# A gated scan feeding a folded multiplicative FFN: PSUM cut into single banks and pairs, two 256-token chunks in front, squares also on ScalarE, and a new order

## The chip, the cores and the metric

One core of a Trainium2 chip runs the whole kernel in one launch. The metric is the device time of an execution in microseconds (us). TensorE (PE) does the matmuls, VectorE (DVE), ScalarE (ACT) and GpSimd (POOL) the elementwise work, and SyncE (SP) issues nearly all transfers.

## The reference, cut to what matters

Inputs are `x`, `r_gate` and `i_gate` of 4 sequences x 5824 tokens x 256 channels, one parameter per channel, and four weight matrices. All are float32.

```python
a_t     = exp(8 * sigmoid(r_gate) * log(clip(sigmoid(a_param))))
norm    = sqrt(max(1 - a_t * a_t, 1e-6))
x_gated = norm * sigmoid(i_gate) * x
h[t]    = a_t[t] * h[t-1] + x_gated[t]            # along the tokens of a sequence, h = 0 at its start
out     = ((h @ w1) * (h @ w2)) @ w3 @ w_out      # w1, w2: 256x1024, w3: 1024x1024, w_out: 1024x256
```

No nonlinear function stands between `w3` and `w_out`, so the kernel multiplies the two matrices first ("the fold") and uses one 1024x256 matrix afterwards.

## The kernel before, in words

The 23296 tokens go in chunks: one of 256 tokens and then 45 of 512 (`sizes`, L50). For each chunk the following steps are done. The letter is the step's name in the order string, with chunk and half or piece behind it (`a7.2` is step a of chunk 7, piece 2).

- `r`, `i`, `x` (`load`, L118): three transfers of tokens by channels.
- `R`, `I` (L126, L136): tanh on ScalarE, from which the sigmoids are made. `p`, `t` (L142, L146): 1 + tanh, and its product with x, on GpSimd or, in one instruction, on VectorE.
- `V`, `U`: turn both results to channels by tokens, through TensorE (`turn_pe`, L162) for the chunks in `TURN_R` and `TURN_U`, else by a transposing DMA on SP's queue (`turn_dma`, L174).
- `d` (`decay`, L181): Exp on ScalarE, 2 halves of 128 channels. `s` (`square`, L190): a_t squared, on GpSimd, or VectorE for `DV_SQUARE`. `q` (`root`, L197): Sqrt on ScalarE. ScalarE loads another function table when it goes from tanh or Exp to Sqrt and back.
- `g` (`gated`, L202) and `h` (`scan`, L214): on VectorE. `y` (`cast`, L229): h in bf16, on GpSimd, or VectorE for `DV_CAST`.
- `a`, `b` (`up`, L240): the products with w1 and w2 in four pieces of 256 of the 1024 columns. A piece has two output banks of PSUM (`[P, 2, CT]`), four matmuls of 512 tokens.
- `c` (`copy`, L256): brings the first product to SBUF in bf16, a piece of 1024 columns per partition in one instruction, on ScalarE or, for `DV_COPY`, VectorE. `m` (`product`, L262): VectorE multiplies it with the second product, which it reads from PSUM.
- `D` (`down`, L269): 128 tokens, 8 matmuls of 256 columns. `e` (`evac`, L280): output from PSUM, on ScalarE or, for `DV_EVAC`, VectorE. `o` (L294): store.

Beside the chunks stand the weights (`Lw..`, `Cw..`: load and cast), the fold (`Ft`, `Fc`, `Fm`, `Fe`, L328 to L372), warm-up matmuls on the identity (`W`, L235, counts in `WARM`), and the decay parameters (`A0.` to `A2.`, L349 to L366): `la4` is read by one DMA as 128 x 2 single elements, and a dozen instructions of two elements each turn it into the scale of the Exp.

PSUM has eight banks here. Six form three pairs in one pool, which `a` and `b` share; two hold outputs, transposes and the fold:

```python
psum   = ctx.enter_context(tc.tile_pool(name="psum", bufs=3, space=bass.MemoryType.PSUM))
psum_o = ctx.enter_context(tc.tile_pool(name="psum_o", bufs=2, space=bass.MemoryType.PSUM))
```

Nothing is scheduled at run time. `ORDER` (L395) is a string of some 2000 words, and the loop behind it issues the steps in that order. Every engine and SP's queue runs its own instructions in the order of the string, and waits only for the data and buffers that it needs.

Of the kernel before, what the change touches and what calls it, by code (L numbers as in the profile page):

```python
# [22 lines left out]
def kernel(  # L23
# [12 lines left out]
    nc = tc.nc  # L36
# [13 lines left out]
    sizes = [256] + [CT] * 45  # L50
# [10 lines left out]
    psum = ctx.enter_context(tc.tile_pool(name="psum", bufs=3, space=bass.MemoryType.PSUM))  # L61
# [6 lines left out]
    la4 = consts.tile([P, NCB], F32, tag="la4")  # L68
    zz, zd, zt = (consts.tile([P, NCB], F32, name=tag, tag=tag) for tag in ("zz", "zd", "zt"))
# [9 lines left out]
    TURN_R = {0, 1, 2, 3, 4, 5, 7, 8, 13}  # L79
    TURN_U = {0, 1, 2, 3, 5, 8, 9}  # L80
    DV_TIMES = {0, 1, 2, 8}
    DV_PLUS = set()
    DV_HALF = set()
    DV_SQUARE = {(0, 0), (0, 1), (1, 0), (1, 1), (5, 0), (6, 0), (7, 1), (9, 1), (11, 0), (12, 0), (14, 0), (15, 1),
        (20, 1), (24, 1), (27, 0), (29, 0), (36, 0), (37, 0), (38, 0), (41, 0)}
    DV_CAST = {0, 20, 28, 37, 39, 40, 42, 45}
    DV_COPY = {(0, 3), (1, 1), (1, 3), (2, 1), (3, 2), (7, 2), (8, 0), (8, 1), (10, 0), (11, 1), (13, 0), (14, 0),
        (14, 2), (15, 3), (18, 1), (18, 3), (19, 3), (20, 3), (21, 3), (22, 3), (23, 1), (25, 0), (25, 2), (28, 1), (33,
        1), (33, 2), (36, 3), (40, 2), (41, 2), (41, 3), (44, 0), (45, 0)}
    DV_EVAC = {(0, 0), (1, 1), (2, 0), (2, 1), (3, 0), (4, 0), (4, 1), (5, 0), (6, 1), (7, 1), (8, 1), (9, 1), (10,  # L90
        0), (17, 0), (18, 1), (19, 0), (19, 1), (22, 0), (23, 1), (27, 0), (27, 1), (28, 1), (30, 0), (31, 0), (33, 1),
        (34, 1), (35, 0), (35, 1), (41, 1), (42, 0), (42, 1)}
    FOLD_ACT = {('c', 7), ('e', 0), ('e', 1), ('e', 4), ('e', 6), ('e', 7)}
    W_ACT = {('w2', 0), ('w3', 1), ('w3', 2), ('w3', 3)}
    W_DVE = {('w3', 0)}
    STAGE = {'w1': ['a', 'a'], 'w2': ['nrm', 'nrm'], 'wo': ['a', 'nrm'], 'w3': ['a', 'nrm', 'a', 'nrm', 'a', 'nrm',
        'a', 'nrm']}
    WARM = [30, 30, 24]
    src = {"r": rf, "i": jf, "x": xf}

    def flat(t):
        return t.rearrange("p cb j q -> p (cb j q)").rearrange("p (j d) -> p j d", d=D)

# [22 lines left out]
    def tanh_r(c):  # L126
        n = sizes[c] // P
        t = gates.tile([P, NCB, 4, P], BF16, name="th_r", tag="th_r")
        if c in TURN_R:
            nc.scalar.activation(out=flat(t)[:, :n, :], in_=T["r", c][:, :n, :], func=AF.Tanh, scale=0.5)  # L130
        else:
            nc.scalar.activation(out=t.rearrange("p cb j q -> p j cb q"), in_=cut(T["r", c]),  # L132
                                 func=AF.Tanh, scale=0.5)
        T["thr", c] = t
# [7 lines left out]
    def plus(c):  # L142
        t = T["thi", c]
        (nc.vector if c in DV_PLUS else nc.gpsimd).tensor_scalar(t, t, 1.0, 1.0, op0=ALU.add, op1=ALU.mult)  # L144

    def times(c, half):  # L146
# [5 lines left out]
        js = slice(0, n) if fused else slice(2 * half, 2 * half + 2)  # L152
        if c in TURN_U:
            u, t, xt = flat(u)[:, js, :], t[:, js, :], xt[:, js, :]
        else:
            u, t, xt = u.rearrange("p cb j q -> p j cb q")[:, js], cut(t)[:, js], cut(xt)[:, js]
        if fused:
            nc.vector.scalar_tensor_tensor(out=u, in0=t, scalar=1.0, in1=xt, op0=ALU.add, op1=ALU.mult)
        else:
            (nc.vector if (c, half) in DV_HALF else nc.gpsimd).tensor_mul(out=u, in0=t, in1=xt)  # L160

# [12 lines left out]
    def turn_dma(c, key, nm):  # L174
        pool, tag = (gates, "rt") if key == "pr" else (held, "ut")
        dst = pool.tile([P, NCB, 4, P], BF16, name=tag, tag=tag)
        nc.sync.dma_start_transpose(out=dst.rearrange("p cb j q -> p (cb j) q"),
                                    in_=T[nm, c].rearrange("p cb j q -> p (cb j q)"))
        T[key, c] = dst.rearrange("p cb j q -> p cb (j q)")
# [10 lines left out]
    def square(c, cb):  # L190
# [3 lines left out]
        eng = nc.vector if (c, cb) in DV_SQUARE else nc.gpsimd  # L194
        eng.tensor_mul(out=T["n", c][:, cb, :w], in0=T["a", c][:, cb, :w], in1=T["a", c][:, cb, :w])  # L195
# [33 lines left out]
    def cast(c):  # L229
        w = sizes[c]  # L230
        T["y", c] = ypool.tile([P, NCB, CT], BF16, name="y_t", tag="y", bufs=4)
        eng = nc.vector if c in DV_CAST else nc.gpsimd
        eng.tensor_copy(out=T["y", c][:, :, :w], in_=T["h", c][:, :, :w])  # L233

    def warm(i):  # L235
        pp = psum.tile([P, 2, CT], F32, name="warm", tag="pab")
# [3 lines left out]
    def up(c, mp, nm, w_sb):  # L240
        w = sizes[c]
        pp = psum.tile([P, 2, CT], F32, name=nm, tag="pab")
        for q in range(2):
            m = 2 * mp + q
            for cb in range(NCB):
                nc.tensor.matmul(out=pp[:, q, :w], lhsT=w_sb[:, cb, m * P:(m + 1) * P],  # L246
                                 rhs=T["y", c][:, cb, :w], start=(cb == 0), stop=(cb == NCB - 1))
        T[nm, c, mp] = pp
# [7 lines left out]
    def copy(c, mp):  # L256
        w = sizes[c]
        sa = ffn.tile([P, 2, CT], BF16, name="sa", tag="sa")
        copy_to((c, mp) in DV_COPY, sa[:, :, :w], T["pa", c, mp][:, :, :w])
        T["sa", c, mp] = sa  # L260
# [54 lines left out]
    def load_w(nm, i):  # L315
        T["wf", nm, i] = held.tile([P, NCB, CT], F32, name="wf", tag=STAGE[nm][i])
# [31 lines left out]

    def rates_abs():  # L349
        nc.vector.scalar_tensor_tensor(out=zz, in0=la4, scalar=-1.0, in1=la4, op0=ALU.mult, op1=ALU.min)  # L350
# [23 lines left out]
    def last(c):  # L374
# [8 lines left out]
        "a": lambda c, mp: up(c, mp, "pa", w1_sb), "b": lambda c, mp: up(c, mp, "pb", w2_sb),  # L383
# [8 lines left out]
        "W": warm, "E": cast_ident, "A0.": rates_abs, "A1.": rates_exp, "A2.": rates,  # L392
# [3 lines left out]
        A0. r1 r0 i0 Lw3.0 x0 i1 A1. E R1 R0 x1 V0 V1 Lw1.1 Cw1.1 I0 A2. d0.0 d0.1 d1.0 d1.1 r2 Lw1.0 Lw2.0 Lw2.1 W1  # L396
        I1 s0.0 Cw3.0 s0.1 t0.1 s1.0 s1.1 W0 U0 i2 Cw1.0 q0 t1.1 g0 h0.0 q1 R2 U1 Lw3.1 h0.1 y0 W2 a0.2 g1 h1.0 c0.2
        V2 x2 h1.1 Lwo.1 Cw2.1 Cw2.0 Lwo.0 Ft0 a0.0 r4 a0.1 d2.0 c0.0 Lw3.2 c0.1 r3 b0.0 b0.1 s2.0 m0.0 m0.1 I2 d2.1
        Lw3.5 y1 Fc0 b0.2 b0.3 m0.2 s2.1 Lw3.4 a0.3 c0.3 m0.3 Cw3.1 Cwo.1 a1.2 Ft1 q2 a1.0 t2.1 Cwo.0 U2 i3 a1.1 c1.2
        b1.0 Fc1 c1.0 g2 c1.1 h2.0 R4 h2.1 m1.0 Lw3.3 Fm1 Fm0 Fe1 Fe0 y2 i4 b1.1 Cw3.5 r6 V4 b1.2 m1.1 m1.2 R3 V3 d4.0  # L400
        d4.1 a1.3 Ft5 d3.0 b1.3 a2.0 d3.1 Cw3.2 Fc5 x3 Ft2 c1.3 s4.0 Cw3.4 s4.1 I3 Lw3.6 Lw3.7 r5 s3.0 x4 s3.1 c2.0
        Fc2 p3 t3.0 I4 Cw3.3 Fm5 R6 i5 t3.1 b2.0 m1.3 Fe5 Cw3.6 p4 Fm2 q3 Ft4 a2.2 Fe2 m2.0 Ft3 Fc4 Fc3 a2.1 c2.1 Fm4
        U3 q4 Fe4 g3 a2.3 c2.2 Fm3 Ft6 r7 R5 Fe3 b2.1 Fc6 Cw3.7 Ft7 V6 r9 Fm6 b2.2 m2.1 Fc7 Fe6 c2.3 Fm7 V5 b2.3 x5
        t4.0 t4.1 I5 U4 Fe7 h3.0 h3.1 D1.0 d5.0 d5.1 R7 D1.1 m2.2 e1.0 y3 R9 m2.3 i6 i7 a3.0 g4 D0.0 h4.0 V7 a3.1 h4.1
        a3.2 p5 d6.0 c3.0 c3.1 d7.0 x6 d7.1 V9 r8 b3.0 I6 D0.1 s5.0 d9.0 d9.1 c3.2 y4 m3.0 e0.0 b3.1 d6.1 R8 b3.2 a4.0
        D1.2 r11 D1.3 m3.1 m3.2 s7.0 a4.1 s5.1 t5.0 p6 t5.1 e1.1 s6.0 c4.0 b4.0 s6.1 U5 s7.1 c4.1 I7 b4.1 o1.0 m4.0
        m4.1 q5 D2.0 D2.1 i8 e2.0 a4.2 a3.3 a4.3 q6 c4.2 b4.2 g5 c3.3 r10 r12 D2.2 b4.3 c4.3 b3.3 q7 h5.0 t6.0 p7 D2.3
        h5.1 R10 m4.2 t6.1 x8 x7 o2.0 U6 o1.1 o0.0 I8 y5 m4.3 m3.3 a5.2 t7.0 e2.1 a5.0 a5.1 V8 c5.2 D3.0 b5.0 c5.0 i9
        V10 g6 t7.1 h6.0 h6.1 c5.1 d8.0 s8.0 d8.1 s9.0 y6 o2.1 U7 x9 b5.1 b5.2 m5.0 D3.1 a5.3 D4.0 m5.1 m5.2 R11 d10.0
        I9 a6.0 e3.0 R12 a6.1 D3.2 V11 c5.3 g7 t8.1 D4.1 h7.0 h7.1 s8.1 D3.3 b5.3 c6.0 i10 b6.0 s9.1 I10 c6.1 e4.0  # L410
        m5.3 e3.1 d10.1 b6.1 m6.0 y7 d11.0 U8 s10.0 s10.1 m6.1 r13 q8 i13 r14 o3.0 p9 r15 g8 h8.0 D4.2 h8.1 a6.2 c6.2
        a6.3 p10 c6.3 q9 V12 o4.0 o3.1 b6.2 D4.3 R13 b6.3 x11 i11 D5.0 D5.1 s11.0 a7.0 m6.2 m6.3 e4.1 b7.0 x10 d12.0
        c7.0 y8 t9.0 t9.1 a7.1 t10.0 e5.0 c7.1 d11.1 b7.1 m7.0 U9 m7.1 D5.2 t10.1 b8.0 a8.0 D5.3 s11.1 x13 I13 R14 I11
        g9 h9.0 c8.0 m8.0 p11 D6.0 a7.2 d12.1 c7.2 i12 r16 U10 D6.1 q11 q10 e5.1 a8.2 a8.1 o4.1 V14 h9.1 c8.1 b8.1
        c8.2 m8.1 V13 b7.2 b8.2 p13 t11.0 t13.0 t13.1 d13.0 R15 a7.3 e6.0 y9 t11.1 m7.2 c7.3 b7.3 m8.2 g10 d13.1 m7.3
        h10.0 D6.2 h10.1 s13.0 a9.0 a9.1 i15 r19 o5.1 R16 V15 U11 o6.0 c9.0 o5.0 D6.3 a8.3 b9.0 d14.0 c9.1 c8.3 b8.3
        I12 s12.0 a9.2 m9.0 i14 x12 y10 d15.0 d14.1 c9.2 d15.1 e6.1 m8.3 b9.1 D7.0 s12.1 r18 U13 o6.1 V16 I15 g11 D7.1
        e7.0 r17 s14.0 m9.1 D7.2 b9.2 p12 s13.1 t12.0 t12.1 x15 x14 o7.0 R19 I14 m9.2 p15 s15.0 a10.0 D7.3 D8.0 d16.0
        b10.0 D8.1 a10.1 e7.1 c10.0 m10.0 a10.3 c10.1 c10.3 b10.1 a10.2 h11.0 m10.1 h11.1 p14 d16.1 D8.2 b10.2 a9.3
# [109 lines left out]
```

## Time and profile before

| what | value |
|---|---|
| time, median of 13 runs | 520.96 us (519.45 to 526.92) |
| time of the profiled execution | 520.45 us |
| its span, first to last instruction | 518.7 us |
| busy: PE / DVE / ACT / POOL | 501.4 / 476.5 / 429.6 / 297.8 us |
| copies of the first product on ACT / DVE | 152 / 32 |
| function table loads on ACT | 40, 1.28 us each |
| transposing DMAs | 76 |
| moved by DMA | 123.28 MB |

Busy time is the time in which an engine has at least one instruction running. Instructions of one engine overlap a little at their ends, so the time from start to start of two instructions in a row is shorter than one of them lasts. Matmuls overlap much: one lasts 377 ns in the mean, and the next starts long before that. `(+1 forms)` in a group means that its mean mixes two shapes.

### The profile page before, as it was taken

How to read it: one execution, taken by the hardware profiler on the slowest of the kernel's cores; microseconds unless marked ns; L12 is line 12 of the kernel's file. 1: busy time of each engine (PE TensorE's matmuls, PEld its weight loads, DVE VectorE, ACT ScalarE, POOL GpSimd, SP SyncE). 2: the span in 40 equal slices, each digit the busy share in tenths (PEclk: the TensorE clock that was granted, in tenths of full speed). 3: DMA queues.
4: the chain of work that ended last, by engine and by line, in shares of the span. 5: the costliest groups of instructions: out<-in, count | busy, mean ns of one | idle time of the engine just before them, and what ended most of it. 6: DMA issues, size and time to landing. Idle time of an engine off the chain costs nothing.

```text
span 518.7 us, 8827 instructions
## 1 busy us (share of the span) xinstructions
PE 501.4 (97%) x3260; PEld 308.7 (60%) x3260; DVE 476.5 (92%) x456; ACT 429.6 (83%) x493; POOL 297.8 (57%) x251
## 2 busy tenths in 40 slices
PE   4899999999999999999999999999999999999997
PEld 4667566556565665566665556666556565566555
DVE  5998999999999999899999899999998998999973
ACT  6999998998898988999987997988977797766432
POOL 0667655777828775876566765756357756634000
PEclk9999999999999999999999999999999999999999
DMA  8999979899999786999979969988967978343113
GB/s 299 404 410 298 378 234 229 277 278 256 336 313 236 205 238 197 279 261 311 232 227 307 234 214 215 306 237 244 237 174 218 259 210 222 102 123 83 61 54 109
DMA packets 174604, 123.28 MB, mean 238 GB/s; under 512 B 84448, under 2 KB 170208, under 8 KB 174560
## 3 DMA queue, kind: packets, MB, share of 16 engines
q1 hardware_dynamic: 174288, 122.71, 83.3%
q8 instruction: 25, 0.41, 0.4%
q14 instruction: 19, 0.16, 0.1%
q10 hardware_dynamic: 272, 0.00, 0.0%
HBM read 78.91 MB, written 23.86 MB: 198 GB/s over the span
## 4 chain that ended last, share of the span: by engine, by line
PE 66%; DVE 14%; DMA 9%; issue 5%; ACT 3%; POOL 2%; SPq 0%; DVEq 0%; ACTq 0%; POOLq 0%
PE po L277 22%; PE pb L246 22%; PE pa L246 21%; DVE g_t L266 6%; DVE h_t L225 4%; DMA x_t<-in_x_dram 2%; DMA r_t<-in_r_gate_dram 2%; DMA wf<-in_moe_w_dram 2%; DVE nrm L210 1%; DVE sa L252 1%; DMA i_t<-in_i_gate_dram 1%; DMA ut<-u_t 1%; ACT a_t L188 1%; POOL u_t L160 1%; DMA la<-in_a_param_dram 1%
## 5 line engine op out<-in xcount | busy, mean ns | idle before, releaser
L246 PEld LDWEIGHTS <-w_sb 128*128 128x128 bf16 x1472 | 142.9, 98 | 150.7 <-issue 10.3
L266 DVE TENSOR_TENSOR g_t<-sa,pb 128x1024 bf16<-128x1024 bf16 (+1 forms) x184 | 216.0, 1199 | 17.0 <-PE pb L246 12.3
L254 ACT CAST sa<-pa 128x1024 bf16<-128x1024 f32 (+1 forms) x152 | 149.5, 1003 | 50.2 <-PE pa L246 46.6
L246 PE MATMUL pb<-y_t,w_sb 128*128 128x512 bf16 (+1 forms) x736 | 180.4, 377 | 3.7 <-DVE sa L252 1.3
L246 PE MATMUL pa<-y_t,w_sb 128*128 128x512 bf16 (+1 forms) x736 | 180.4, 377 | 2.8 <-DVE g_t L266 1.0
L277 PE MATMUL po<-wp_sb,g_t 128*128 128x256 bf16 x1456 | 179.4, 273 | 0.0
L277 PEld LDWEIGHTS <-g_t 128*128 128x128 bf16 x1456 | 142.3, 98 | 42.5 <-issue 0.2
L225 DVE TENSOR_TENSOR_SCAN h_t<-a_t,h_t,nrm 128x512 f32<-128x512 f32 (+3 forms) x90 | 116.7, 1322 | 1.2
L160 POOL TENSOR_TENSOR u_t<-th_i,x_t 128x512 bf16<-128x512 f32 x84 | 113.4, 1366 | 2.2 <-DMA ut<-u_t 0.9
L233 POOL CAST y_t<-h_t 128x1024 bf16<-128x1024 f32 x38 | 44.4, 1169 | 118.5 <-DVE h_t L225 92.4
L195 POOL TENSOR_TENSOR nrm<-a_t 128x512 f32<-128x512 f32 x72 | 85.2, 1196 | 18.1 <-ACT a_t L188 17.9
L144 POOL TENSOR_SCALAR th_i<-th_i 128x1024 f32<-128x1024 f32 x42 | 47.8, 1142 | 31.1 <-ACT th_i L139 31.1
L188 ACT ACTIVATE a_t<-rt,la 128x512 f32<-128x512 bf16 x74 | 59.1, 819 | 2.6 <-DMA rt<-th_r 1.5
L139 ACT ACTIVATE th_i<-i_t 128x1024 f32<-128x1024 f32 (+1 forms) x46 | 48.3, 1052 | 9.7 <-DMA i_t<-in_i_gate_dram 6.6
L210 DVE SCALAR_TENSOR_TENSOR nrm<-nrm,ut 128x1024 f32<-128x1024 f32 x39 | 52.7, 1353 | 1.2 <-DMA ut<-u_t 1.2
L254 ACT COPY ot<-po 128x512 f32<-128x512 f32 (+1 forms) x60 | 34.6, 577 | 17.3 <-PE po L277 16.2
L199 ACT ACTIVATE nrm<-nrm 128x1024 f32<-128x1024 f32 (+1 forms) x46 | 46.9, 1048 | 0.3
L252 DVE CAST sa<-pa 128x1024 bf16<-128x1024 f32 (+1 forms) x32 | 38.3, 1197 | 5.6 <-PE pa L246 5.5
L132 ACT ACTIVATE th_r<-r_t 128x1024 bf16<-128x1024 f32 x37 | 39.2, 1061 | 0.1
L199 ACT ACT_TABLE_LOAD x20 | 25.7, 1283 | 1.6 <-DVE nrm L195 1.2
L252 DVE COPY ot<-po 128x512 f32<-128x512 f32 (+1 forms) x33 | 21.8, 664 | 3.8 <-PE po L277 3.8
L195 DVE TENSOR_TENSOR nrm<-a_t 128x512 f32<-128x512 f32 (+1 forms) x20 | 17.8, 898 | 0.9 <-ACT a_t L188 0.9
(51 smaller groups left out, 153.2 us busy)
## 6 DMA issues: line engine op xcount, KB each, us to landing
r_t<-in_r_gate_dram SPq DMA_DIRECT2D x45, 512.0 KB, 5.4
i_t<-in_i_gate_dram SPq DMA_DIRECT2D x45, 512.0 KB, 5.4
x_t<-in_x_dram SPq DMA_DIRECT2D x45, 512.0 KB, 5.6
out_dram<-ot SPq DMA_DIRECT2D x89, 256.0 KB, 3.8
wf<-in_moe_w_dram SPq DMA_DIRECT2D x12, 512.0 KB, 9.3
wf<-in_moe_w_out_dram SPq DMA_DIRECT2D x2, 512.0 KB, 10.6
ut<-u_t SPq DMA_TRANSPOSE x39, 5.2
rt<-th_r SPq DMA_TRANSPOSE x37, 4.4
```

Source lines behind the costliest of these rows:

```text
L139: nc.scalar.activation(out=t[:, :n, :], in_=T["i", c][:, :n, :], func=AF.Tanh, scale=0.5)
L160: (nc.vector if (c, half) in DV_HALF else nc.gpsimd).tensor_mul(out=u, in0=t, in1=xt)
L188: nc.scalar.activation(out=a, in_=pr, func=AF.Exp, scale=la4[:, cb:cb + 1], bias=la4[:, cb:cb + 1])
L195: eng.tensor_mul(out=T["n", c][:, cb, :w], in0=T["a", c][:, cb, :w], in1=T["a", c][:, cb, :w])
L199: nc.scalar.activation(out=T["n", c][:, :, :w], in_=T["n", c][:, :, :w], func=AF.Sqrt, scale=-1.0, bias=1.0)
L210: nc.vector.scalar_tensor_tensor(out=T["n", c][:, :, :w], in0=T["n", c][:, :, :w], scalar=1e-3, in1=T["pu", c][:, :, :w], op0=ALU.max, op1 ...
L225: nc.vector.tensor_tensor_scan(T["h", c][:, cb, lo:hi], T["a", c][:, cb, lo:hi], T["n", c][:, cb, lo:hi], init, ALU.mult, ALU.add)
L246: nc.tensor.matmul(out=pp[:, q, :w], lhsT=w_sb[:, cb, m * P:(m + 1) * P], rhs=T["y", c][:, cb, :w], start=(cb == 0), stop=(cb == NCB - 1))
L252: nc.vector.tensor_copy(out=dst, in_=src_ps)
L254: nc.scalar.copy(out=dst, in_=src_ps)
L266: nc.vector.tensor_mul(out=T["g", c][:, 2 * mp:2 * mp + 2, :w], in0=T["sa", c, mp][:, :, :w], in1=T["pb", c, mp][:, :, :w])
L277: nc.tensor.matmul(out=po, lhsT=T["g", c][:, k, j * P:(j + 1) * P], rhs=wp_sb[:, k, :], start=(k == 0), stop=(k == KD - 1), skip_group_che ...
```

## The change

- **Chunks**: 256, 256, then 44 of 512, and 256 at the end. `dense` packs the short chunks for the transposing DMA.
- **PSUM**: the first product gets two single banks (`psum_a`), the second two pairs (`psum_b`). Outputs keep two. `a` and `c` are now steps of one bank each: two matmuls and a copy of 512 columns.
- **Assignments**: `AC_SQUARE` puts 17 squares on ScalarE, and VectorE keeps one of 20. `DV_COPY`, `DV_EVAC` and `DV_CAST` name only steps of chunks 0 to 10, 0 to 9 and 0, so later copies and outputs are ScalarE's and later casts GpSimd's. `AC_CAST` puts the cast of chunk 1 on ScalarE.
- **Turns**: fewer chunks go through TensorE (72 matmuls, not 120), so more by DMA (83 transfers, two of them short, not 76).
- **Decay parameters**: read as two rows of 128 elements, turned by one small TensorE transpose, and copied from PSUM by VectorE.
- **Warm-up matmuls**: 26 + 10 + 20, not 30 + 30 + 24.
- **Order**: a new string throughout.

By the built instruction streams ScalarE has 323 copies of 512 columns and 16 of 256 for the first product, 82 output copies and 34 table loads. VectorE has 37 copies of the first product and 10 output copies.

```diff
-    sizes = [256] + [CT] * 45
+    sizes = [256, 256] + [CT] * 44 + [256]
...
-    psum = ctx.enter_context(tc.tile_pool(name="psum", bufs=3, space=bass.MemoryType.PSUM))
+    psum_a = ctx.enter_context(tc.tile_pool(name="psum_a", bufs=2, space=bass.MemoryType.PSUM))
+    psum_b = ctx.enter_context(tc.tile_pool(name="psum_b", bufs=2, space=bass.MemoryType.PSUM))
...
-    TURN_R = {0, 1, 2, 3, 4, 5, 7, 8, 13}
-    TURN_U = {0, 1, 2, 3, 5, 8, 9}
-    DV_TIMES = {0, 1, 2, 8}
+    TURN_R = {0, 1, 2, 3, 4, 7, 9}
+    TURN_U = {0, 1, 2, 3}
+    DV_TIMES = {0, 1}
...
+    AC_SQUARE = {(2, 1), (3, 0), (4, 0), (5, 0), (7, 0), (8, 0), (9, 1), (10, 0), (10, 1), (12, 1), (13, 0), (13, 1),
+        (14, 0), (14, 1), (15, 0), (15, 1), (16, 0)}
+    DV_CAST = {0}
+    AC_CAST = {1}
...
-    WARM = [30, 30, 24]
+    WARM = [26, 10, 20]
...
-        eng = nc.vector if (c, cb) in DV_SQUARE else nc.gpsimd
-        eng.tensor_mul(out=T["n", c][:, cb, :w], in0=T["a", c][:, cb, :w], in1=T["a", c][:, cb, :w])
+        n, a = T["n", c][:, cb, :w], T["a", c][:, cb, :w]
+        if (c, cb) in AC_SQUARE:
+            nc.scalar.activation(out=n, in_=a, func=AF.Square)
+        else:
+            (nc.vector if (c, cb) in DV_SQUARE else nc.gpsimd).tensor_mul(out=n, in0=a, in1=a)
...
+    def up(c, m, dst, w_sb):
+        w = sizes[c]
+        for cb in range(NCB):
+            nc.tensor.matmul(out=dst[:, :w], lhsT=w_sb[:, cb, m * P:(m + 1) * P],
+                             rhs=T["y", c][:, cb, :w], start=(cb == 0), stop=(cb == NCB - 1))
+
+    def up_a(c, mp, q):
+        T["pa", c, mp, q] = pp = psum_a.tile([P, CT], F32, name="pa", tag="pa")
+        up(c, 2 * mp + q, pp, w1_sb)
+
+    def up_b(c, mp):
+        T["pb", c, mp] = pp = psum_b.tile([P, 2, CT], F32, name="pb", tag="pb")
         for q in range(2):
...
+            up(c, 2 * mp + q, pp[:, q, :], w2_sb)
...
-    def copy(c, mp):
-        w = sizes[c]
-        sa = ffn.tile([P, 2, CT], BF16, name="sa", tag="sa")
-        copy_to((c, mp) in DV_COPY, sa[:, :, :w], T["pa", c, mp][:, :, :w])
-        T["sa", c, mp] = sa
+    def copy(c, mp, q):
+        w = sizes[c]
+        if q == 0:
+            T["sa", c, mp] = ffn.tile([P, 2, CT], BF16, name="sa", tag="sa")
+        copy_to((c, mp, q) in DV_COPY, T["sa", c, mp][:, q, :w], T["pa", c, mp, q][:, :w])
...
+    def rates_turn():
+        pt = psum_b.tile([P, 2, CT], F32, name="pr_la", tag="pb")
+        nc.tensor.matmul(out=pt[:, 0, :NCB], lhsT=la_rows, rhs=ident_f[:NCB, :NCB], is_transpose=True,
+                         start=True, stop=True)
+        T["la"] = pt[:, 0, :NCB]
+
     def rates_abs():
+        nc.vector.tensor_copy(out=la4, in_=T["la"])
...
-    nc.scalar.dma_start(out=la4, in_=a_param.rearrange("(cb p) -> p cb", p=P))
+    nc.scalar.dma_start(out=la_rows, in_=a_param.rearrange("(cb p) -> cb p", p=P))
```

The beginning of the new order, up to the first product with w1, reads:

```
r0 r1 E i0 A3. A0. A1. A2. x0 R0 R1 I0 Lw1.0 i1 Lw2.0 t0.1 x1 r2 W0 r3 V0 d0.0 d0.1 s0.0 s0.1 V1 d1.0 s1.0
d1.1 s1.1 q0 W1 U0 W2 g0 h0.0 h0.1 Cw2.0 y0 Cw1.0 a0.0.0 a0.0.1 q1 Lw1.1 Lw2.1 I1 t1.1 U1 g1 h1.0 ...
```

The old one reads:

```
A0. r1 r0 i0 Lw3.0 x0 i1 A1. E R1 R0 x1 V0 V1 Lw1.1 Cw1.1 I0 A2. d0.0 d0.1 d1.0 d1.1 r2 Lw1.0 Lw2.0 Lw2.1 W1
I1 s0.0 Cw3.0 s0.1 t0.1 s1.0 s1.1 W0 U0 i2 Cw1.0 q0 t1.1 g0 h0.0 q1 R2 U1 Lw3.1 h0.1 y0 W2 a0.2 ...
```

## The prediction

> **What bounds the kernel now.** I read the page first, then busy time by stage, then the timeline of the start and of one stretch in the middle, and last the chain.
>
> The page: engine, busy time, share of the span, instructions; then the chain that ended last, by engine; then groups of instructions (busy, mean ns of one | idle before them).
>
> ```profile
> PE 501.4 (97%) x3260; PEld 308.7 (60%) x3260; DVE 476.5 (92%) x456; ACT 429.6 (83%) x493; POOL 297.8 (57%) x251
> ...
> PE 66%; DVE 14%; DMA 9%; issue 5%; ACT 3%; POOL 2%; SPq 0%; DVEq 0%; ACTq 0%; POOLq 0%
> ...
> L266 DVE TENSOR_TENSOR g_t<-sa,pb 128x1024 bf16<-128x1024 bf16 (+1 forms) x184 | 216.0, 1199 | 17.0 <-PE pb L246 12.3
> L254 ACT CAST sa<-pa 128x1024 bf16<-128x1024 f32 (+1 forms) x152 | 149.5, 1003 | 50.2 <-PE pa L246 46.6
> ...
> L254 ACT COPY ot<-po 128x512 f32<-128x512 f32 (+1 forms) x60 | 34.6, 577 | 17.3 <-PE po L277 16.2
> ```
>
> TensorE is nearly full, VectorE is next, and ScalarE has 89 us to spare. Busy time by stage (stretch: length, then busy time of PE, PEld, DVE, ACT, POOL, clock, DMA share, GB/s):
>
> ```profile
> 16.00:26.00 10.00, 8.60 (x77) 5.96 (x78) 9.70 (x14) 9.88 (x13) 7.67 (x7) 1.00 1.06 404
> 26.00:78.00 52.00, 51.71 (x390) 33.45 (x389) 49.28 (x53) 51.02 (x60) 34.17 (x31) 1.00 1.02 330
> ...
> 130.00:442.00 312.00, 308.85 (x1895) 185.03 (x1894) 295.51 (x263) 272.12 (x309) 198.37 (x161) 1.00 0.90 245
> 442.00:519.00 77.00, 73.50 (x468) 45.48 (x465) 62.36 (x56) 38.96 (x47) 19.36 (x16) 1.00 0.31 90
> ```
>
> Up to 78 us ScalarE and the DMA engines are full; from 130 us on TensorE is, with VectorE at 295.5 of 312. Now the start (start, duration, engine, line), and two lines of the chain for TensorE's pace:
>
> ```profile
> 5.45 0.20 ACT L354 ACTIVATE zz<-zz 128x2 f32<-128x2 f32 x1 [2.94 <-DVE zz L350]
> ...
> 8.43 4.74 PE L238 MATMUL warm<-ident 128*128 128x128 bf16 x60
> ...
> 13.68 1.50 PE L238 MATMUL warm<-ident 128*128 128x128 bf16 x24
> ...
> 16.04 0.60 PE L246 MATMUL pa<-y_t,w_sb 128*128 128x256 bf16 x4 [0.86 <-DVE y_t L233]
> ...
> 18.82 1.07 ACT L254 CAST sa<-pa 128x512 bf16<-128x512 f32 x2
> ...
> 24.91 1.91 ACT L254 CAST sa<-pa 128x1024 bf16<-128x1024 f32 x2
> ```
> ```profile
> 148.37 1.75 PE po L277 x16
> 150.12 1.73 PE pa L246 x8
> ```
>
> Paces: an up matmul of 512 columns 1.73/8 = 0.216 us, a down one of 256 1.75/16 = 0.109 (also an up one of 256: 0.60 us for four, less the 0.27 that one lasts), a 128-column one 0.056 (24 in 1.50 us, one lasting 0.22). From the first up matmul on, TensorE owes 1440 x 0.216 + 32 x 0.109 + 1456 x 0.109, plus the fold of w3 with w_out (64 x 0.056 + 64 x 0.109), plus 96 transposes x 0.056 = 489.2 us. So the span splits as 16.0 (first up matmul) + 489.2 + 3.4 (from the last matmul to the end) + 10.1 of waits = 518.7. The run took 520.45, 1.75 more than its span; the median of all runs is 520.96. Only the 16.0, the transposes and the 10.1 can be won.
>
> **TensorE.** By the instruction order 1408 up matmuls have 512 columns and 96 have 256, which is the same sum of columns to 0.1 us; transposes fall from 120 to 72, 16 of them ahead of the first up matmul: 56 x 0.056 remain behind it. The debt becomes 487.0, -2.2 us. What is turned by DMA instead goes from 76 to 83 transfers on SP's queue; there one holds the queue for 1.25 us ("SPq L177 DMA_TRANSPOSE ut<-u_t" at 46.52). Two more fall into the first 60 us, where DMA is full, with the loads of chunks 7 to 9 behind them. Those loads are ordered several chunks ahead, so I charge nothing; without that cover it is 2.5 us.
>
> **The start.** Ahead of the first root ScalarE now has chunk 1 with 256 tokens, not 512: a tanh falls from 1.06 to 0.61 and two Exps from 0.80 to 0.56 each (-0.9 us), and chunk 1's tanh of the input gate (1.06) goes behind the roots. That is 2.0 us. On VectorE the cast of w2's first half now stands between scan and y: +0.6 (row of the weight casts, 0.69 less overlap). Squares of chunk 0 go from VectorE to GpSimd, 0.55 us each by half of 1.04; the table load and chunk 1's Exps (2.2 us) cover them. The decay parameters come as two rows of 512 B, not 256 elements of 4 B; the old load landed at 5.25 and held ScalarE's first tanh until 5.56. How early the new one and r0 land no row shows: not before 2.4 (0.73, plus 1.7 for the 128 KB store, the shortest transfer here), not after 5.25. The new TensorE turn and VectorE copy take some 0.5 of it. I take 1.2 us earlier, bounds -0.5 to 2.4. Together 2.6, say 2.5 (0.9 to 3.8): the first up matmul at 13.5.
>
> The Trainium skill ("TensorE: Matmul & The Clock Gate", part 1 on the clock gate) speaks against this edit. Row first: the profile's granted clock reads 1.00 for 0 to 10 us, yet the 60 warm-up matmuls at 8.43 take 4.74 us, 0.079 each, and the 24 at 13.68 take 0.056 each. The page says that the array runs at half rate until some 3.4 us of sustained work, and falls back after such a time idle. Warm-ups fall from 84 to 56 and the last 20 are issued with chunk 0's turn of u, so a gap of 4 us may precede the first up matmul. By the page its first 3.4 us would then run at half pace, 1.7 us lost on TensorE; the row alone says 0. I keep 0, since ScalarE and DMA set this stage.
>
> **ScalarE and VectorE.** Back to back, a copy of 512 columns starts 1.07 - 0.58 = 0.49 us after the last, one of 1024 1.91 - 1.01 = 0.90. The up copies of ScalarE go from 149 wide and 3 half ones (135.6 us) to 323 of 512 and 16 of 256 (162.6): +27.0. Evacuations 58 to 81 x 0.49: +11. Squares 17 x 0.53: +9.0. Smaller ones +0.7. Table loads 40 to 34 x 1.29: -7.8. Sum +40: 430 becomes 470. VectorE loses 15 us of copies, 15 of evacuations, 17 of squares and 5 of casts, and gains 3 in gating and weights: 476 becomes about 427. So VectorE is freed everywhere and ScalarE becomes the second engine. In the middle one chunk costs ScalarE ten copies x 0.49, three gate functions x 0.95, two Exps x 0.71 and 0.7 table loads, 10.1 us, and TensorE 32 x 0.216 + 32 x 0.109 = 10.4.
>
> Where ScalarE is worst is found by adding its work along the new order. Up to chunk 7's first product: 30 gate functions x 0.95, 6 halves, 24 Exps, 8 squares, 24 copies and evacuations of 512 and 8 of 256, 10 table loads and 6 us of weights, fold and y make 85 us (each start to start, so 0.1 under its row), from a start at 4.3. TensorE then still owes 419 of 491 and 3.4: the span can't be under 511. The same sum before also gives 511, at chunk 2, and 518.7 was measured: a floor, not a forecast.
>
> **Banks.** One wide copy freed two banks; now each frees its own, and TensorE can be two single products ahead of ScalarE. In the new order at least 1.3 us of other TensorE work, in the median 2.2, stands between a bank's last matmul and its next use, against 0.58 for a copy. Hence no charge while ScalarE keeps its place. Of the 10.1 us of waits I take away 3 that VectorE causes (it releases most TensorE waits that the view of waits names) and add 3.8 for a ScalarE that is full up to 150 us: 10.9. Bounds 6 and 21 (the slower rival).
>
> **Sum.** 13.5 + 487.0 + 10.9 + 3.4 = 514.8; with the 1.75 around the span 516.5 us, 0.8% under the median.
>
> **Rivals.** *Slower: copies queue behind table loads.* 67 up copies stand in ScalarE's order behind more than 1.2 us of other work; a table load and a root are 2.25, with the copy 2.8. Against that 15 of them have 1.3 us of cover and 24 have 2.2: 15 x 1.5 + 24 x 0.6 = 37 us short, if ScalarE always came just in time. If it does so for one in four, 9 us: 525.5. From one in nine the gain is spent, from one in five it is slower by over 0.5%. For it: ScalarE has 0.3 us per chunk left. Against: today 46.6 us of its waits are for pa, so it tends to be early.
>
> *No change.* The floor is 511 as before; if the 7.7 us between floor and span stay too, the time is 518.7 + 1.75 = 520.5. For it: ScalarE fills 51.0 of 52 us there already and gets more. Against: VectorE's part of the waits goes.
>
> *The start doesn't move*, because DMA, full from 10 us, sets the first product, not ScalarE: 514.8 + 2.5 + 1.75 = 519.0.
>
> **How the numbers follow.** Forecast 0.52, all of it faster; no change 0.16 and unmoved start 0.10, both within 0.5% (2.6 us, about what a measurement of this kernel can tell from none); slower 0.22. The range: 511 is a start 3.8 us earlier with 6.7 of waits, 524.5 takes in a good part of the slower rival. The forecast's own range is 511 to 518.3.
>
> **What would show it.** Right: first up matmul at 12.5 to 14.5; ACT 460 to 475 us busy, DVE 415 to 440; PE as busy as now in 130 to 442. The banks: waits of pa matmuls for ACT's sa copies, under 1 us in sum if I am right, over 6 if the rival is. Wrong: ACT idle in the first 100 us beyond 5 us, or TensorE matmuls of 256 columns at 0.2 us after the start.

## The result, and the profile after

The changed kernel takes **525.33 us** (median of 11 runs, 523.56 to 528.43) against 521.02 us of the kernel before (48 runs): a ratio of **1.0084, 95% interval 1.0063 to 1.0105**. It is slower by 0.8%; 516.5 us and a gain had been forecast. Its profiled execution took 523.73 us, with a span of 521.9 us.

Page of the changed kernel: busy time of the engines, the granted clock in 40 slices, the chain by engine, and the two groups that answer to those of before (busy, mean ns | idle before them):

```profile
PE 502.6 (96%) x3217; PEld 309.2 (59%) x3217; DVE 441.7 (85%) x420; ACT 467.0 (89%) x717; POOL 326.4 (63%) x269
...
PEclk9799999999999999999999999999999999999999
...
PE 63%; DMA 11%; DVE 10%; ACT 7%; issue 5%; POOL 2%; SPq 1%; DVEq 0%; ACTq 0%; POOLq 0%
...
L288 DVE TENSOR_TENSOR g_t<-sa,pb 128x1024 bf16<-128x1024 bf16 (+1 forms) x188 | 218.2, 1176 | 57.9 <-PE pb L260 39.1
...
L276 ACT CAST sa<-pa 128x512 bf16<-128x512 f32 (+1 forms) x339 | 186.1, 584 | 34.7 <-PE pa L260 29.7
```

ScalarE is at 467 us, and VectorE waits 39.1 us for second products in front of its gating products, before 12.3: by the whole run, the load moved as intended. By stage (length, then busy PE, PEld, DVE, ACT, POOL, clock, DMA share, GB/s) it did not:

```profile
10.00:16.00 6.00, 2.58 (x19) 1.79 (x19) 5.51 (x12) 5.36 (x7) 0.94 (x1) 0.81 1.03 411
16.00:26.00 10.00, 9.25 (x77) 6.91 (x74) 7.96 (x15) 9.29 (x14) 8.48 (x9) 0.77 1.05 404
26.00:78.00 52.00, 48.48 (x356) 31.06 (x357) 50.05 (x63) 50.15 (x69) 35.81 (x31) 1.00 1.12 330
78.00:130.00 52.00, 50.06 (x300) 28.96 (x298) 50.55 (x51) 50.58 (x74) 33.55 (x29) 1.00 1.07 290
130.00:442.00 312.00, 309.31 (x1899) 185.03 (x1897) 271.63 (x219) 297.39 (x460) 226.07 (x175) 1.00 0.92 248
```

The kernel before, in the one of these stages that the prediction doesn't show:

```profile
78.00:130.00 52.00, 50.72 (x329) 30.96 (x327) 50.65 (x49) 46.27 (x54) 36.19 (x31) 1.00 1.01 261
```

Between 26 and 78 us TensorE is busy 48.5 us, before 51.7; VectorE is as full as before (50.05 against 49.28), and so it is from 78 to 130 (50.55 against 50.65). ScalarE is full in both stages now (50.2 and 50.6; before 51.0 and 46.3). Apart from 16 to 26 us (7.96, before 9.70), VectorE has become free only behind 130 us (271.6, before 295.5), where TensorE was the bound anyway.

The start (start, duration, engine, line; in brackets the idle time before):

```profile
12.63 0.60 PE L260 MATMUL pa<-y_t,w_sb 128*128 128x256 bf16 x4 [4.14 <-DVE y_t L250]
13.23 0.40 PE L177 MATMUL ptr<-ident,u_t 128*128 128x128 bf16 x4
13.71 1.03 PE L177 MATMUL ptr<-ident,th_r 128*128 128x128 bf16 x8
15.45 0.58 PE L260 MATMUL pa<-y_t,w_sb 128*128 128x256 bf16 x2 [0.71 <-DVE sa L274]
...
18.81 2.01 PE L260 MATMUL pa<-y_t,w_sb 128*128 128x256 bf16 x8
...
27.12 0.62 PE L177 MATMUL ptr<-ident,th_r 128*128 128x128 bf16 x8 [1.60 <-ACT th_r L137]
```

The first up matmul is 3.4 us earlier (12.63 for 16.04). After 4.1 idle us the granted clock falls: eight transposes take 1.03 us from 13.71 and 0.62 at 27.12, eight up matmuls of 256 columns 2.01 us, some 0.23 each.

By the prediction's split the span is now 12.6 (first up matmul) + 487.2 (debt) + 18.7 (waits) + 3.4 (tail). The waits, worked out from each matmul's start less the pace of the one before it, by stage:

| stage, us | before | after |
|---|---|---|
| first up matmul to 28 | 2.0 | 6.6 |
| 28 to 60 | 1.0 | 3.4 |
| 60 to 130 | 2.2 | 4.5 |
| 130 to the end | 4.8 | 4.2 |
| sum | 10.1 | 18.7 |

TensorE's earliest possible end (the time plus what it still owes) is 4.4 us ahead of before at 12.6 us, the start and most of the smaller debt together. The lead is 0.8 at 28 us and gone at 40; at 130 us TensorE is 3.7 us behind. Which waits: up to 28 us the slow clock (2.4), the transposes of chunk 4 for ScalarE's tanh (2.0) and VectorE's copies (1.7); from 28 to 60 us mostly the fold (1.9 of the 3.4 at its steps or for its results); from 60 to 130 us VectorE's gating products (2.2) and copies (2.0).

The same waits, sorted by the engine whose work the trace names as released last, with the slow clock on its own:

| waits of TensorE, us | before | after |
|---|---|---|
| VectorE, up to 130 us | 2.2 | 7.7 |
| VectorE, behind 130 us | 4.5 | 1.1 |
| ScalarE | 1.9 | 5.5 |
| slow clock | 0 | 2.4 to 2.6 |
| GpSimd | 1.6 | 1.3 |

### The profile page after: what moved, and what is told of

Its sections match the earlier page's. It is cut to its first block, busy times and chain, and to the rows that moved or that the text cites. A ratio compares the mean times of both kernels' runs of the same rounds, so it can differ in the third digit from the quotient of the medians.

```text
span 521.9 us, 8939 instructions
## 1 busy us (share of the span) xinstructions
PE 502.6 (96%) x3217; PEld 309.2 (59%) x3217; DVE 441.7 (85%) x420; ACT 467.0 (89%) x717; POOL 326.4 (63%) x269
## 4 chain that ended last, share of the span: by engine, by line
PE 63%; DMA 11%; DVE 10%; ACT 7%; issue 5%; POOL 2%; SPq 1%; DVEq 0%; ACTq 0%; POOLq 0%
PE po L299 22%; PE pb L260 21%; PE pa L260 20%; DVE g_t L288 4%; DVE h_t L239 4%; DMA i_t<-in_i_gate_dram 3%; DMA ut<-u_t 2%; DMA r_t<-in_r_gate_dram 2%; ACT sa L276 2%; DMA rt<-th_r 2%; DMA out_dram<-ot 1%; POOL u_t L170 1%; DVE sa L274 1%; DMA x_t<-in_x_dram 1%; SPq L128 1%
## 5 line engine op out<-in xcount | busy, mean ns | idle before, releaser
L288 DVE TENSOR_TENSOR g_t<-sa,pb 128x1024 bf16<-128x1024 bf16 (+1 forms) x188 | 218.2, 1176 | 57.9 <-PE pb L260 39.1
L276 ACT CAST sa<-pa 128x512 bf16<-128x512 f32 (+1 forms) x339 | 186.1, 584 | 34.7 <-PE pa L260 29.7
L170 POOL TENSOR_TENSOR u_t<-th_i,x_t 128x512 bf16<-128x512 f32 (+1 forms) x89 | 124.4, 1416 | 10.9 <-DMA ut<-u_t 5.5
L239 DVE TENSOR_TENSOR_SCAN h_t<-a_t,h_t,nrm 128x512 f32<-128x512 f32 (+4 forms) x92 | 127.6, 1403 | 1.6
L250 POOL CAST y_t<-h_t 128x1024 bf16<-128x1024 f32 (+1 forms) x45 | 52.9, 1175 | 96.9 <-DVE h_t L239 85.9
L209 POOL TENSOR_TENSOR nrm<-a_t 128x512 f32<-128x512 f32 (+1 forms) x76 | 86.6, 1152 | 10.2 <-ACT a_t L199 9.9
L151 POOL TENSOR_SCALAR th_i<-th_i 128x1024 f32<-128x1024 f32 (+1 forms) x45 | 58.4, 1300 | 47.2 <-ACT th_i L146 47.2
L199 ACT ACTIVATE a_t<-rt,la 128x512 f32<-128x512 bf16 (+1 forms) x80 | 64.7, 822 | 0.3 <-DMA rt<-th_r 0.3
L224 DVE SCALAR_TENSOR_TENSOR nrm<-nrm,ut 128x1024 f32<-128x1024 f32 (+1 forms) x43 | 58.0, 1350 | 3.8 <-DMA ut<-u_t 2.7
L276 ACT COPY ot<-po 128x512 f32<-128x512 f32 x82 | 48.2, 594 | 9.8 <-PE po L299 7.7
L139 ACT ACTIVATE th_r<-r_t 128x1024 bf16<-128x1024 f32 (+1 forms) x40 | 42.6, 1064 | 0.8 <-DMA rt<-th_r 0.4
```

Source lines behind the costliest of these rows:

```text
L199: nc.scalar.activation(out=a, in_=pr, func=AF.Exp, scale=la4[:, cb:cb + 1], bias=la4[:, cb:cb + 1])
L209: (nc.vector if (c, cb) in DV_SQUARE else nc.gpsimd).tensor_mul(out=n, in0=a, in1=a)
L224: nc.vector.scalar_tensor_tensor(out=T["n", c][:, :, :w], in0=T["n", c][:, :, :w], scalar=1e-3, in1=T["pu", c][:, :, :w], op0=ALU.max, op1 ...
L239: nc.vector.tensor_tensor_scan(T["h", c][:, cb, lo:hi], T["a", c][:, cb, lo:hi], T["n", c][:, cb, lo:hi], init, ALU.mult, ALU.add)
L276: nc.scalar.copy(out=dst, in_=src_ps)
L288: nc.vector.tensor_mul(out=T["g", c][:, 2 * mp:2 * mp + 2, :w], in0=T["sa", c, mp][:, :, :w], in1=T["pb", c, mp][:, :, :w])
```

## The experiments

Each ratio is to the kernel before, measured beside it; the changed kernel itself has 1.0084.

### The first doubts: clock, banks, swapped work

**The cold clock.** Edit of the changed kernel: `WARM = [26, 10, 20]` becomes `[26, 10, 92]`.

> The changed kernel with 92 warm-up matmuls in place of 20 behind chunk 0's turn of u, so that TensorE has work until shortly before its first up matmul at 12.6 us. Clock theory (the idle 4 us ahead of that matmul put the granted clock at half from 13.6 to 20.6 us): clock 1.00 in 10 to 26 us, eight 256-column matmuls in 1.0 us and not 2.0, and 2 to 4 us less, some 522 us. Rival (weights and ScalarE set this stage, the slow matmuls fill waits): clock 1.00 as well, but the work that is late at 28 us is late still, 524.5 to 525.5 us. Bank theory: nothing changes behind 28 us, where 12 of the 18.6 us of waits lie.

Measured: 525.51 us, 1.0079 [1.0052, 1.0106]. The first up matmul comes at 12.40 without the idle time, and the clock falls for about half as long, though it still does:

```profile
10.00:16.00 6.00, 4.39 (x60) 3.68 (x58) 5.51 (x11) 5.09 (x6) 0.90 (x1) 0.96 1.04 412
16.00:26.00 10.00, 8.48 (x75) 6.38 (x72) 7.95 (x16) 9.40 (x15) 8.58 (x9) 0.86 1.05 406
```

TensorE works less in 16 to 26 (8.48 for 9.25), that is, it waits instead: its waits up to 28 us come to 6.8 us, in the changed kernel to 6.6. The half clock is real, and the half of it that this run takes away was worth nothing. No run took away all of it.

**Single banks in the old order.** Edit of the kernel before: pools, `up_a`, `up_b` and narrow copies as in the change, and 333 steps put off until a bank is free.

> The kernel before with the change's PSUM part: copies of 512 columns, two single banks for the first product, two pairs for the second. Chunks, assignments and order stay, but for the products that now have to wait until the copy two banks earlier has been issued: 333 of some 2800 words go a few places back. Bank theory (the single banks make TensorE wait for copies, 6.5 us in the changed kernel): waits of pa matmuls for sa copies of several us, 525 us or more, against 521.7 with narrow copies in pairs. Rival (the banks are covered wherever an order leaves room; ScalarE's load is the cause): 521 to 523 us.

**Narrow copies alone**, the pairs kept: `copy` of the kernel before issues two copies of 512 columns.

> The kernel before with every copy of a pair done as two copies of 512 columns one after the other, on the same engine, banks still pairs, order unchanged. It shows what the narrower copies alone cost: 152 x 0.07 us more on ScalarE and 32 x 0.06 on VectorE. If ScalarE's extra 10 us is hidden: 521 us within 0.7. If the engines' fullness up to 130 us passes it on: 523 to 525 us.

Measured: 566.26 us, 1.086 [1.0843, 1.0878], and 521.74 us, 1.0006 [0.9991, 1.0021]. That there are twice as many copies costs nothing that this shows. Banks that the order was not made for, with the steps put off for them, cost 45 us, and the view of TensorE's waits in that run says where (microseconds in sum, times, longest):

```profile
PE pa L244 <- ACT sa L260: 18.7, 39, 1.4
PE pa L244 <- DVE sa L258: 9.2, 13, 1.9
```

**Pairs in the new order.** Edit of the changed kernel: `psum_a` goes, `psum_b` has three pairs for both products, 444 steps are put off.

> The changed kernel with PSUM as before: three pairs that first and second products share; the copies stay narrow and on the same engines, and 444 words of the order are put off to the next place at which a pair is free. Theory B (the cut into single banks costs, the rest of the change gains): 518 to 522, with no waits of pa matmuls for copies over 1 us in sum. Theories A and C (the load up to 130 us costs, banks nothing): 525 to 528. A rival: the new order was made for single banks as the old one was for pairs, and putting steps off costs by itself: 540 or more, and then nothing is learned of the banks but that order and banks go together.

Measured: 592.93 us, 1.1368 [1.1338, 1.1398]. The rival of the last sentence holds: order and banks go together, and undoing either tells nothing of what the banks cost in their own order.

**Swapped work back.** Edit of the changed kernel: `DV_COPY` keeps only chunks 0 to 4 (16 copies go to ScalarE), `AC_SQUARE = set()` (17 squares go to GpSimd).

> The changed kernel with the 16 first-product copies that VectorE does in chunks 5 to 10 on ScalarE, and the 17 squares that ScalarE does on GpSimd; order unchanged. Bank theory (TensorE waits for a single bank because VectorE comes late to copy it): of the 4.5 us that TensorE waits between 60 and 130 us the 2.0 put down to VectorE's copies go, 523 us. ScalarE theory (ScalarE is full up to 130 us and any copy there comes late): ScalarE's load is about even (16 x 0.47 on, 17 x 0.53 off), so waits for its copies take the place of the others, 525 us.

**Copies to VectorE in the middle.** Edit: the copies `(c, 3, 1)` of chunks 11 to 40 are VectorE's, which is free there.

> The changed kernel with one of the eight copies of each of chunks 11 to 40 on VectorE (which is idle for 40 of 312 us from 130 us on) in place of ScalarE. ScalarE theory for the middle: part of the 4.2 us of TensorE's waits behind 130 us goes, 1 to 3 us less. Rival (by then ScalarE's slack is enough, and a copy on VectorE is later than one on ScalarE): 525 to 527 us.

Measured: 529.16 us, 1.0158 [1.0129, 1.0187], and 544.63 us, 1.0444 [1.0407, 1.0481], both above everything that was expected. Thirty copies of 0.68 us, on an engine with 40 us of room, cost 19 us. TensorE's waits for the gating products (1.9 us in the changed kernel) and for ScalarE's copies (1.4) grow most in the second kernel:

```profile
PE pb L261 <- DVE g_t L289: 12.1, 15, 3.0
PE pa L261 <- ACT sa L277: 6.4, 10, 1.9
```

My reading, which no run tests, is that an added copy holds up the work that stands behind it in VectorE's order.

### Load up to 130 us

**ScalarE relieved**: the root reads the decay where ScalarE squared it.

```diff
-        if (c, cb) in AC_SQUARE:
-            nc.scalar.activation(out=n, in_=a, func=AF.Square)
-        else:
+        if (c, cb) not in AC_SQUARE:
```

> The changed kernel without the 17 squares on ScalarE (left out, not moved: the root reads the decay itself there; nine roots fall into two halves for it). ScalarE has 7.9 us less to do in chunks 2 to 16 and no other engine has more. ScalarE theory (it is full from 16 to 130 us, idle 8 of 114 us there, and what it does late is late for good): TensorE is 4 to 7 us further at 130 us, and the time 520 to 522 us. Bank theory: waits for copies depend on who comes when, at most 2 us less, 523.5 to 525.5 us.

**VectorE relieved**: its copies of chunks 5 to 10 are cut to 64 columns, which their products read eight times over.

> The changed kernel, but the 16 copies that VectorE still does in chunks 5 to 10 read 64 of their 512 columns, and the products of these pieces read the 64 columns eight times over. What is left out is 7/8 of these copies; order, banks and ScalarE's work stay. It takes some 16 x 0.45 = 7 us off VectorE, all before 130 us. Theory A (VectorE, whose work up to 130 us the change didn't cut, sets the lag there): the lag of 3.7 us that TensorE has at 130 us goes, 519.5 to 522. Theory B (a single bank waits for whichever engine copies it, and the order has no slack for that): only the waits for VectorE's own copies shrink, 523.5 to 525.5. Theory C (both engines are full, neither alone is worth anything): 525 to 526, as it was for ScalarE without its squares.

**Both relieved.**

> The changed kernel with both reliefs: the 17 squares of ScalarE left out (the root reads the decay in their place) and the 16 copies of VectorE in chunks 5 to 10 cut to 64 of 512 columns. ScalarE has 7.9 us less, VectorE 7 us less, both before 130 us; order and banks stay. Theory A and theory C (the load of the two engines up to 130 us is what makes it slow): 516.5 to 520, and TensorE's earliest possible end at 130 us falls from 514.2 to 511 or less. Theory B (banks and order, whatever the load): 523 to 525.5.

**Squares out, and the 16 copies given to ScalarE.**

> The changed kernel with the 17 squares of ScalarE left out and the 16 copies of VectorE in chunks 5 to 10 given to ScalarE: ScalarE's work up to 130 us is as in the changed kernel to 0.1 us, VectorE's is 9.6 us less, GpSimd's the same. Theory A (VectorE sets the lag): 520 to 522.5. Theory C (both are full): 524 to 526. Theory B (a copy that changes its engine under single banks stands where the order doesn't expect it): 527 to 530, with waits of pa matmuls for ScalarE's copies of 4 us or more between 60 and 130 us, as when copies and squares were both moved.

Measured: 527.15 us, 1.0109 [1.0091, 1.0128]; 524.02 us, 1.0051 [1.0029, 1.0072]; 524.30 us, 1.0050 [1.0028, 1.0071]; 528.87 us, 1.0145 [1.0108, 1.0183]. ScalarE's squares are worth nothing, alone or on top. VectorE's copies are worth some 1.7 us of the 4.4 (the intervals overlap a little, so less is possible), and giving them to ScalarE loses more than that. But this relief begins at 73 us, and 14 of the 16 copies lie behind 78; the stages of the kernel with both:

```profile
26.00:78.00 52.00, 48.36 (x360) 31.55 (x365) 51.31 (x65) 49.07 (x68) 36.25 (x32) 1.00 1.09 329
78.00:130.00 52.00, 51.00 (x310) 30.57 (x315) 46.90 (x53) 46.79 (x68) 32.73 (x30) 1.00 1.06 296
```

Before 78 us, where most of the lag arises, VectorE stayed as full as it was (51.3 of 52). No run relieved it ahead of 73 us.

### The tie of TensorE to its copies

**First and second try**: the first product goes to a bank that nobody reads, and the copies read one that is filled once (`pc`). In the first try each product takes that bank anew; in the second it is held all along (`px`).

```diff
-        T["pa", c, mp, q] = pp = psum_a.tile([P, CT], F32, name="pa", tag="pa")
+        pp = T["px"]
...
-        copy_to((c, mp, q) in DV_COPY, T["sa", c, mp][:, q, :w], T["pa", c, mp, q][:, :w])
+        copy_to((c, mp, q) in DV_COPY, T["sa", c, mp][:, q, :w], T["pc"][:, :w])
```

> The changed kernel with TensorE and the copies of the first product taken apart: all first products go to one bank that nobody reads, and the copies, the same ones on the same engines, read another bank that is filled once at the start. What is left out is that the copies bring the first product; order, widths, loads and the banks of the second product stay. TensorE then never waits for a copy, and the copies never wait for TensorE. Theory B (single banks tie TensorE to the engine that copies, and this is what costs): the 6.5 us of waits of pa matmuls go and the copies run ahead, 517 to 520. Theory A/C (load of VectorE and ScalarE up to 130 us): waits of pa turn into waits of pb for gating and products, 523 to 525. Theory D (the lead of the start was worth little from the outset, since ScalarE and the transfers set when chunk 2 is ready): up to 28 us nothing gets better, 522 to 524.

> The same, and also the 17 squares of ScalarE left out and the 16 copies of VectorE in chunks 5 to 10 cut to 64 of 512 columns: no tie between copies and TensorE, and 7 to 8 us less for either engine up to 130 us. Theory B alone: as the run without the cut, to 0.5 us. If tie and load both count: 514.5 to 518, below each alone. Theory D: what stays above 512 is the start's, and TensorE's earliest possible end at 28 us is still 506 or more.

> The kernel before with TensorE and the copies of the first product taken apart in the same way: first products to one bank that nobody reads, wide copies from another that is filled once, the second product on two pairs of its own. It tells what the tie costs in the kernel before. If the shared pairs cost it little: 517.5 to 520.5, and the gain is smaller by 3 us or more than in the changed kernel. If the two kernels gain alike, the tie isn't what tells them apart.

Measured: 543.47 us, 1.0426 [1.0400, 1.0451]; with the cuts 540.18 us, 1.0374 [1.0351, 1.0397]; the kernel before 571.75 us, 1.0978 [1.0957, 1.0999]. All theories missed: the edit put in a wait of TensorE for earlier matmuls of its own, some 0.2 to 0.27 us at a time, wherever the bank is taken anew:

```profile
201.95 0.59 PE L264 MATMUL pa<-y_t,w_sb 128*128 128x512 bf16 x2 [0.27 <-PE pb L264]
```

With the bank held:

> The changed kernel with the first product and its copies taken apart, without the fault of the first try: the bank that nobody reads is held for the whole run, so that no matmul waits for TensorE's own earlier ones (there this wait cost some 0.22 us each time, 14 us of TensorE's time between 130 and 442 us alone). TensorE waits for no copy, copies wait for no matmul of the first product; order, widths, loads, second product as in the changed kernel. What is left out is that the copies bring the first product. Theory B (the tie through single banks costs): 517 to 520.5. Theory A/C (load): the waits go over to the second product, 523 to 525. Theory D (the start's lead is worth nothing; it is lost by 28 us): TensorE's earliest end at 28 us no better than in the changed kernel, and the time 520 to 524, according to what the tie takes after that.

> The kernel before, taken apart in the same way, the unread bank held for the whole run, two pairs for the second product alone. Before, no first product waited for a copy and the second product's waits for copies were 2.5 us in sum. If the tie tells the two kernels apart: 517.5 to 520.5, a gain of at most 3 us, smaller than that of the changed kernel. If it gains as much as the changed kernel or more, the tie isn't the difference. With two pairs rather than three for the second product it may also lose: over 522.

Measured: 526.67 us, **1.0101 [1.0083, 1.0118]**, and 538.12 us, 1.0332 [1.0316, 1.0347]. The first is above every range that was expected. In the changed kernel no matmul of a first product waits for a copy any more, and it is no faster. The view of its TensorE waits:

```profile
PE pb L265 <- DVE g_t L293: 5.6, 10, 1.2
...
PE pa L265 <- POOL y_t L250: 2.1, 2, 1.9
PE ptr L177 <- ACT th_r L137: 1.7, 1, 1.7
...
PE po L304 <- ACT ot L281: 1.5, 1, 1.5
```

The 6.5 us of waits for copies (2.8 for ScalarE's, 3.7 for VectorE's) have turned into waits for the gating products, the casts of h and the evacuations. So taking the tie to the single banks away gains nothing by itself; that the banks have no part in it isn't shown, since other waits took the place of these. In the kernel before, the missing third pair made the second product wait 15.7 us for gating (1.1 before), so that run does not price the tie there.

### The start

**Rows alone in the kernel before**: `la_rows` and `A3.` as in the change.

> The kernel before with one part of the change alone: decay parameters read as two rows and turned by TensorE. If the parameters held the start: first tanh at 4 to 4.5 us and not 5.56, first up matmul 1 us earlier, 520 us. If the loads of r hold it as well (here 512 tokens of chunk 1 come first): no change, 521 us within 0.5.

**Rows undone in the changed kernel.**

> The changed kernel with the decay parameters read as 256 single elements, as before, in place of two rows, and without the small turn: the first up matmul goes about 1 us back, from 12.6 to 13.5 or later. In the kernel before the two rows brought 0.7 us at the first up matmul and 1.1 us of time. Theory D (in the changed kernel the lead of the start is lost by 28 us whatever it was): 525 to 526, no change. Otherwise, lead one to one: 526.2 to 527.

Measured: 520.18 us, **0.9975 [0.9960, 0.9991]**, faster than both kernels; and 525.56 us, 1.0087 [1.0065, 1.0108]. In the first, the first up matmul comes at 15.33, 0.7 earlier, and the time falls by about 1.1. In the second ScalarE's first tanh starts at 4.62, not 3.41, the first up matmul at 13.81, and the time stays. So 1.2 us of the changed kernel's lead at the start show no worth, though the interval leaves room for about 1 us of it.

**The late copies of the best kernel to ScalarE**: the rows, and all copies and evacuations from chunk 27 on ScalarE's.

> The kernel before with two parts of the change: decay parameters as rows, and from chunk 27 on all copies and evacuations on ScalarE (9 wide copies and 12 evacuations leave VectorE, order unchanged). If the 4.8 us that TensorE waits behind 130 us are VectorE's fullness, as the releasers say, 2 to 4 us go: 516.5 to 518.5 us. If they are the order's and not the load's: 520 us, as with the rows alone.

Measured: 521.64 us, 1.0010 [0.9998, 1.0023]. Relieving VectorE late gains nothing either; the rows alone had 0.9975 [0.9960, 0.9991], so it takes their gain away.

## Why the prediction was wrong, point by point

**The start: right in size, wrong in worth.** 2.5 us (0.9 to 3.8) was forecast and 3.4 came; the decay parameters had landed by 2.2 us, a little before the 2.4 that was taken for the earliest. But the sum took the lead over to the end. As I read the trace, the rival "the start doesn't move" had the reason, at the wrong place: it is not the first product that ScalarE and the transfers hold, but the next chunk. The timeline of ScalarE, changed kernel, then kernel before:

```profile
23.11 1.06 ACT L213 ACTIVATE nrm<-nrm 128x1024 f32<-128x1024 f32 x1
```
```profile
23.95 1.06 ACT L199 ACTIVATE nrm<-nrm 128x1024 f32<-128x1024 f32 x1
```

The root of chunk 2 comes only 0.84 us earlier. Until then two chunks of 256 tokens give TensorE 512 tokens to work on, where the kernel before had 768. Counted from the traces, matmuls of both up products worth 400 tokens had started by 26 us and 480 by 30, before 464 and 592. The earlier start is spent in waiting.

**The step that failed: the waits, and in them VectorE's.** 10.9 us were forecast, "3 that VectorE causes" taken away and 3.8 added for ScalarE; 18.7 came. By the second table, ScalarE's 3.8 came out in size (3.6), partly by luck: it was put down to a ScalarE that is full up to 150 us, and 2.2 of it stand behind 160 us. Behind 130 us VectorE's waits did fall by 3.4. But up to 130 us they rose by 5.5, which the sum did not have, and the slow clock, put at 0, makes up most of the rest. The ground was "VectorE is freed everywhere", read from sums over the whole run. By stage it is false. The groups of VectorE's copies of the first product in 26 to 78 us, before and after:

```profile
L252 DVE CAST sa<-pa 128x1024 bf16<-128x1024 f32 x4 | 4.9, 1213 | 0.0
```
```profile
L274 DVE CAST sa<-pa 128x512 bf16<-128x512 f32 x15 | 10.0, 680 | 0.0
```

And in 78 to 130 us, before and after:

```profile
L252 DVE CAST sa<-pa 128x1024 bf16<-128x1024 f32 x4 | 4.8, 1204 | 0.0
```
```profile
L274 DVE CAST sa<-pa 128x512 bf16<-128x512 f32 x14 | 9.3, 679 | 0.2
```

All of the 37 copies left to VectorE lie in chunks 0 to 10, which the list in the change had shown; the 6.8 us of squares that it gave away between 26 and 130 us are outweighed by 9.6 us more of copies. By 78 us VectorE has scanned 2816 tokens, before 3328. From the runs, the copies of chunks 5 to 10 are worth some 1.7 us. What the rest of the lag comes from, the copies in chunks 0 to 4, the places of the steps in the new order, the two short chunks in front or the turns given to DMA, no run tells apart: why TensorE has to wait longer for VectorE there stays open.

**Second engine.** ACT 467.0 lies in 460 to 475. DVE 441.7 misses 415 to 440 and the 427 of the sum: 10.9 of the 15 us are scans (116.7 us before, 127.6 now; last section).

**Banks.** "No charge" is not refuted, and the test it named left it open: waits of pa for ScalarE's copies came to 2.8 us in sum, between the 1 and the 6, and 3.7 more for VectorE's. With all of these taken away the time is no shorter. The slower rival gave 525.5, the measured time, by luck: of its 9 us of waits the trace shows 2.8, and taking them away doesn't help.

**The clock gate.** The Trainium skill ("TensorE: Matmul & The Clock Gate", part 1) was right that the clock would fall, and the row's 0 for it wrong: the granted clock reads 0.81 and 0.77, some 7 us at half. The 1.7 us estimated from the page are 2.4 in the trace's waits. The run with more warm-ups took half of the slow time away and gained nothing, so that half cost nothing in the end, as others set this stage; for the other half no run shows it.

**The turns.** The sum charged nothing for the turns given to DMA, at 1.25 us of SP's queue each. From 26 to 130 us the traces have 15 of them before and 20 after, and they hold the queue for 27.4 and 43.0 us. The waits of the engines that end with a turn's landing are 2.1 and 3.3 us there, so not much of the lag shows as such a wait; but no run gave the turns back.

**The rest held**: debt 487.2 (12 transposes stand ahead of the first up matmul, not 16, which is 0.2 us) and tail 3.4; the floor of 511 was not touched; behind 130 us TensorE is as busy as before. Both observations named as "wrong" in advance came: matmuls of 256 columns at 0.2 us after the start, and ScalarE idle for 6.7 us of the first 100, though before it was 8.5.

## What to carry to other kernels

An engine's load is to be summed by stage before it is called freed: here VectorE lost 35 us over the run and none from 26 to 130 us, where it was full. A lead at the start need not reach the end: look also at the second round of the slowest stage, not only at the first product. And in an order written out for given banks and engines, a copy is not moved for its duration's worth: here thirty of them cost 19 us, and taking one kind of wait away handed it to the next step.

## What the runs showed of the hardware

VectorE's scans last longer beside GpSimd work. In 130 to 442 us there are 54 of 512 columns in both kernels, before and after:

```profile
L225 DVE TENSOR_TENSOR_SCAN h_t<-a_t,h_t,nrm 128x512 f32<-128x512 f32 x54 | 71.3, 1347 | 1.0
```
```profile
L239 DVE TENSOR_TENSOR_SCAN h_t<-a_t,h_t,nrm 128x512 f32<-128x512 f32 x54 | 82.1, 1534 | 0.9
```

Over the run, scans of this size with GpSimd work beside at most a fifth of them last 1.27 us in both traces (1.25 to 1.28; 67 before, 49 after); with it beside nine tenths or more they last 1.82 and 1.78 us in the mean, 7 before and 23 after. The change gives GpSimd 28.6 us more. The Trainium skill ("SBUF — State Buffer", the section on two separate sides) says that a VectorE operation with two SBUF inputs and a GpSimd operation that reads SBUF contend for a shared pair of ports, an exclusive lock, and that the one that comes second waits. The durations agree with it; no run tested the lock itself.

The clock fell after short gaps as well: in the run with 92 warm-ups eight transposes took 0.61 us at 13.24 and 1.06 at 16.97, with 1.37 us of idle time between them.
